# Retention and two routed expert layers on one core: output scaling and half of the masks move to ScalarE and GpSimd, logits are issued later, and SyncE's queue in the expert part is reordered

## The chip, the cores and the metric

The kernel runs on one core of one Trainium2 chip, as one program in one launch. The metric is device time in microseconds (us) of an execution; less is better. The engines of the core are TensorE (PE in the rows; PEld is its weight loads), VectorE (DVE), ScalarE (ACT), GpSimd (POOL) and SyncE (SP), which only issues DMAs. SBUF is the memory on the chip, PSUM the accumulators that matmuls write.

## The reference

Three layers follow each other: a retention without softmax, a layer of 8 experts, and a second layer of 8 experts. Each of the 4608 rows goes through one expert of each layer, chosen by the largest logit.

```python
# q, k, v: (B=8, H=8, S=576, 64) f32
scores = (1/8) * q @ k.T;  gamma_h = 1 - 2**(-5-h)
ret = scores * where(i >= j, gamma_h ** (i-j), 0)
x = (ret @ v), laid out as rows (B*S = 4608, D = 512)
# twice, with 8 experts, w1 (512, 1024), w2 (1024, 512):
logits = x @ w_gate          # the second layer adds modality_bias[modality_id]
e = argmax(logits);  p = softmax(logits)[e]
y = p * (relu(x @ w1[e]) @ w2[e])   # the first layer times sigmoid(x @ w_output_gate)[e] too
x = y
```

## The kernel before, in words

**Stage 1, attention and routing** (`attention_and_routing`). Retention is computed by chunks of 128 positions with a state per head. A batch element has four chunks and a half one; two elements share the half chunks as one joint tile, the tail. So there are 4 pairs x (4 + 4 + 1) = 36 chunks of 128 rows. For each chunk these steps run (names of `PLAN`, engine and line in brackets): the scaling of v (`vs`, GpSimd, L264); the scores of eight heads in two PSUM tiles `pa` of 128x512 (`S`, TensorE, L272); the product of q with the old state (`qS`, TensorE, L304); the new state's product (`kv`, TensorE, L279); the causal mask on each of the two score tiles (`am0`, `am1`, VectorE, L319); the state (`Sb`, VectorE, L288); the products of masked scores and v (`av0`, `av1`, TensorE, L304); the scaling of the output by a factor per row and head (`out`, VectorE, L326); the sum of squares of a row (`sq`, ScalarE, L330); a power of two from it as the row's scale (`rs1`, `rs2`, VectorE, L336 and L340); the row in float16 (`xh`, ScalarE, L345) and its rest in float16 (`xl`, VectorE, L348), which also issues a DMA transposition into `xT` on SyncE; and the router's logits from the transposed row (`lg`, TensorE, L357).

`PLAN` gives each step a time in chunks, counted from the chunk's own index; the program sorts all steps of all chunks by that time and emits them in this order, and each engine runs its own in order. Four to five chunks form a group of routing: when its last logits are due, `route` (VectorE mostly, with exponentials on ScalarE) steps forward every `STEP` of a chunk, and then GpSimd scatters the group's rows into the experts' buckets in DRAM (L170). Tiles of q, k, v are loaded by SyncE 4.5 chunks ahead, 256 KB each. `WEIGHTS` gives the times at which the 16 pieces (256 KB each, 128x512 float32) of the first expert's weights are converted, by ScalarE (L432) and VectorE (L433), into two float16 planes: the number and its rest. Their loads go through SyncE from chunk 30.3 on.

**Between the stages** the counts per expert go to registers (L405 to L415), a barrier waits for the scatters, and `experts` starts.

**Stage 2, the experts** (`experts`). Each engine has a program of its own, written out, with semaphores (`take` waits and counts down). The loop goes over 16 expert layers P, 8 of the first and 8 of the second layer. The rows of an expert come in slots: slot 0 and slot 1 are units of two blocks of 128 rows, then possibly more, then one odd block. For a unit SyncE transposes the rows into `xT` (L788), TensorE multiplies by the first weights (L947 to L949, three products of float16 planes), ScalarE and VectorE apply relu and split the result (L1046, L1155), TensorE multiplies by the second weights (L955 to L957), and ScalarE scales. In the first layer the rows of a finished block become rows `x2row`, SyncE transposes them to `x2T` (`turn`, L775), and in a later unit TensorE computes the second router's logits from them (L926), between the four quarters of the first product. The weights of the next expert come by SyncE (`load_w`, L760, four pieces of 1 MB into `stg`) and are converted by ScalarE (L1023) and VectorE (`stt`, shown with its helper's line L463) while this expert's products run. GpSimd scatters the rows of the second layer. At the start GpSimd clears the planes of `hT` (L1278).

SyncE's queue for an expert P is: slot 0's transposition, the `turn` of finished rows, slot 0's metadata; two pieces of the next expert's weights (`next_w(P+1, 1)`); then the same for slot 1, and so on; and at the end two pieces for the expert after (`next_w(P+2, 0)`).

## Time and profile before

| | |
|---|---|
| median of 3 runs | 1089.32 us (1088.02 to 1094.48) |
| the profiled execution | 1091.79 us, its span 1090.1 us |
| TensorE busy | 1003.2 us, 92% of the span |
| VectorE busy | 508.0 us, 47% |
| ScalarE busy | 329.5 us, 30% |
| GpSimd busy | 207.9 us, 19% |
| moved by DMA | 154.31 MB, 142 GB/s on average |
| mean granted TensorE clock | 0.964 |

All durations below are from the one profiled execution. A row of the timeline is one instruction, or a run of equal ones: start in us, duration in us, engine, line of the kernel, operation, output <- inputs, size, and how many (x16 are sixteen). What stands in brackets is how long the engine was idle before it, and what released it. The granted clock (PEclk) is a share of full speed: 1.00 is 2.4 GHz, 0.50 is 1.2 GHz. Stage 1 fills the first 247 us of the span, the first expert layer goes on to some 715 us, the second to the end.

### The profile page before, as it was taken

The page shows a single profiled execution, that of the slowest core. Times are in us where ns is not written, and L with a number is a line of the kernel's source. Part 1 is how long each engine was busy: PE and PEld are TensorE (multiplying, and loading weights), DVE is VectorE, ACT ScalarE, POOL GpSimd, SP SyncE. Part 2 cuts the span into 40 slices and gives each one's busy share as a digit, 9 for nine tenths or more (in the row PEclk, how much of TensorE's full clock was granted, in tenths as well). Part 3 has the DMA queues.
Part 4 walks back from the last instruction along what each step waited for, and adds up shares of the span by engine and source line. Part 5 has one row for each costly group of instructions (what it writes and reads, how often), then busy time and mean ns, then how long its engine had stood idle before and what let it go on. Part 6 is the DMA issues. An engine that isn't in the chain of part 4 may idle for free. (4 is left out here: it accounts for less than half of the span.)

```text
span 1090.1 us, 23903 instructions
## 1 busy us (share of the span) xinstructions
PE 1003.2 (92%) x8501; PEld 723.0 (66%) x8501; DVE 508.0 (47%) x1560; ACT 329.5 (30%) x637; POOL 207.9 (19%) x245
## 2 busy tenths in 40 slices
PE   7988988817999999999999899999999999999996
PEld 6977877705666767676666576766766766677664
DVE  5578798864555464646465646422311112111111
ACT  2222222332444443434344344313311121112111
POOL 4133333241111121212121213111001110110010
PEclk9799999957999999999999999999999999999998
DMA  9899999947765757574656584345122021311200
GB/s 292 233 251 269 257 273 281 278 128 228 197 152 144 156 134 167 133 157 125 162 136 153 135 167 134 80 135 134 49 59 58 29 61 40 63 55 39 58 29 32
DMA packets 218225, 154.31 MB, mean 142 GB/s; under 512 B 174665, under 2 KB 174829, under 8 KB 218096
## 3 DMA queue, kind: packets, MB, share of 16 engines
q1 hardware_dynamic: 209136, 124.09, 47.2%
q0 software_dynamic: 8960, 28.62, 7.5%
q8 instruction: 67, 1.10, 0.4%
q14 instruction: 62, 0.51, 0.2%
HBM read 80.21 MB, written 33.92 MB: 105 GB/s over the span
## 5 line engine op out<-in xcount | busy, mean ns | idle before, releaser
L947 PE MATMUL ph<-xT,wb 128*128 128x256 f16 (+2 forms) x1344 | 338.9, 263 | 19.7 <-PEq L451 19.7
L949 PE MATMUL ph<-xT,wb 128*128 128x256 f16 (+2 forms) x1344 | 339.0, 263 | 0.0
L948 PE MATMUL ph<-xT,wb 128*128 128x256 f16 (+2 forms) x1344 | 339.0, 263 | 0.0
L1155 DVE SCALAR_TENSOR_TENSOR hT<-ph,hT 128x512 f16<-128x512 f32 (+2 forms) x168 | 106.4, 637 | 333.7 <-DVEq L451 333.6
L955 PE MATMUL py<-wb,hT 128*128 128x512 f16 x608 | 230.6, 379 | 1.3 <-PEq L451 0.6
L956 PE MATMUL py<-wb,hT 128*128 128x512 f16 x608 | 230.5, 379 | 0.0
L957 PE MATMUL py<-wb,hT 128*128 128x512 f16 x608 | 230.4, 379 | 0.0
L1046 ACT ACTIVATE hT<-ph 128x512 f16<-128x512 f32 (+2 forms) x168 | 92.9, 553 | 224.2 <-ACTq L451 224.1
L947 PEld LDWEIGHTS ph<-xT,wb 128*128 128x128 f16 x1344 | 131.6, 98 | 37.6 <-issue 20.6
L948 PEld LDWEIGHTS ph<-xT,wb 128*128 128x128 f16 x1344 | 131.6, 98 | 17.0
L949 PEld LDWEIGHTS ph<-xT,wb 128*128 128x128 f16 x1344 | 131.7, 98 | 12.9
L957 PEld LDWEIGHTS py<-wb,hT 128*128 128x128 f16 x608 | 59.5, 98 | 72.0 <-issue 0.3
L955 PEld LDWEIGHTS py<-wb,hT 128*128 128x128 f16 x608 | 59.3, 98 | 66.9 <-issue 1.6
L956 PEld LDWEIGHTS py<-wb,hT 128*128 128x128 f16 x608 | 59.4, 98 | 64.9
L1273 POOL DMA_INDIRECT out_dram<-yo,idxo x37 | 36.0, 972 | 335.4 <-POOLq L451 322.3
L304 PE MATMUL po<-vs,a 128*128 128x64 f32 x576 | 80.5, 290 | 12.7 <-DVE a L319 12.4
L463 DVE SCALAR_TENSOR_TENSOR wb<-stg,wb 128x2048 f16<-128x2048 f32 x36 | 82.4, 2290 | 11.0 <-DVEq L451 11.0
L304 PEld LDWEIGHTS po<-vs,a 128*128 128x128 f32 x576 | 73.2, 202 | 15.8 <-DVE a L319 15.5
L1040 ACT ACTIVATE yo<-py,v_gcol 128x512 f32<-128x512 f32 x37 | 25.4, 687 | 168.3 <-ACTq L451 168.3
L1262 POOL TENSOR_SCALAR idx<-v_pos 128x1 int32<-128x1 f32 x39 | 10.5, 270 | 334.5 <-POOLq L451 334.5
L1023 ACT ACTIVATE wb<-stg 128x2048 f16<-128x2048 f32 x36 | 68.5, 1902 | 0.0
L319 DVE TENSOR_TENSOR a<-pa,mc 128x512 f32<-128x512 f32 x64 | 43.7, 685 | 42.1 <-PE pa L272 41.8
(154 smaller groups left out, 928.9 us busy)
## 6 DMA issues: line engine op xcount, KB each, us to landing
stg<-in_moe_w_dram SPq DMA_DIRECT2D x36, 1024.0 KB, 8.2
dkn<-in_dk_dram SPq DMA_DIRECT2D x36, 256.0 KB
qn<-in_q_dram SPq DMA_DIRECT2D x36, 256.0 KB
vn<-in_v_dram SPq DMA_DIRECT2D x36, 256.0 KB
kn<-in_k_dram SPq DMA_DIRECT2D x36, 256.0 KB
w0s<-in_moe_w_dram SPq DMA_DIRECT2D x16, 256.0 KB
xs<-zero SPq DMA_DIRECT2D x8, 262.0 KB, 2.2
xs<-zero SPq DMA_DIRECT2D x8, 258.0 KB, 2.8
```

Of the source, the lines that this page charges most:

```text
L304: nc.tensor.matmul(o, a, b_, start=m in fresh, stop=ends.get(m) == n)
L319: nc.vector.tensor_tensor(d4, s4, self.causal(), op=ALU.mult)
L463: r = fn(*a, **kw).then_inc(self.sem, 1)
L947: pe.matmul(o, w1(P_, 0)[:, c, fs], xT[s][:, c, cs], start=(c == 0), stop=False)
L948: pe.matmul(o, w1(P_, 0)[:, c, fs], xT[s][:, 4 + c, cs], start=False, stop=False)
L949: m = pe.matmul(o, w1(P_, 1)[:, c, fs], xT[s][:, c, cs], start=False, stop=(c == 3))
L955: pe.matmul(py[b], hT[:, 0, f, bs], w2(P_, 0)[:, f, :], start=(f == 0), stop=False)
L956: pe.matmul(py[b], hT[:, 0, f, bs], w2(P_, 1)[:, f, :], start=False, stop=False)
L957: m = pe.matmul(py[b], hT[:, 1, f, bs], w2(P_, 0)[:, f, :], start=False, stop=(f == 7))
L1023: ac.activation(wb[P_ % 2][:, 0, 2048 * c:2048 * c + 2048], stg[:, 2048 * c:2048 * c + 2048], AF.Copy, scale=WS).then_inc(T["cv_full"])
L1046: ac.activation(hT[:, 0, 2 * g:2 * g + 2, cs], ph[g][:, :, cs], AF.Relu).then_inc(T["hh_full"])
L1155: stt(hT[:, 1, 2 * g:2 * g + 2, cs], ph[g][:, :, cs], 0.0, hT[:, 0, 2 * g:2 * g + 2, cs], op0=ALU.max, op1=ALU.subtract).then_inc(T["h_full"])
```

## The change

It has four parts.

1. *Stage 1, engines.* `out` becomes eight ScalarE instructions, one per head, 128x64 each, that read the product in PSUM and scale by the head's column of factors. The mask of the second score tile (`am1`, not in tails) becomes a ScalarE copy out of PSUM and a GpSimd AFFINE_SELECT in place (`cut`), which fills zeros above the diagonal; tails and the first score tile keep the multiplication. The exponent `iv` is computed for a group in `route` instead of for each chunk.
2. *Stage 1, order.* `am1`, `out`, `sq`, `rs1` and `lg` have other times; `lg` moves from 3.6 to 4.1.
3. *Between the stages.* Only the first weights of expert 0 are loaded and converted in stage 1. The second weights follow in stage 2: SyncE loads them in two pieces of 1 MB behind the first unit's transposition, ScalarE and VectorE convert them in unit 0 after its first two quarters, and TensorE waits for each (`w0_full2`, `w0_full3`). SyncE issues the first transposition before it reads its other registers. TensorE runs 11 matmuls of constants (`READY`) ahead of the experts. The steps of the second router, which had nothing to do in the first unit, are left out there, with the clearing that they needed.
4. *Stage 2, SyncE's queue.* Slot 1's transpositions come ahead of `next_w(P+1, 1)`. For expert 0, two pieces of expert 1 go out ahead of slot 1 and two behind it, and the writes of padding come after slot 2. The counting of rows for the order of the second layer stands behind the second product instead of within it.

```diff
 PLAN = {
-    "vs": -1.3, "S": 0.0, ... "am0": 0.2, "am1": 0.35, "Sb": 0.5, "av0": 0.8, "av1": 0.85, "out": 1.25,
-    "sq": 1.3, "rs1": 1.65, "rs2": 1.75, "xh": 1.8, "xl": 2.25, "lg": 3.6,
+    "vs": -1.3, "S": 0.0, ... "am0": 0.2, "am1": 0.25, "cut": 0.4, "Sb": 0.5, "av0": 0.8, "av1": 0.85, "out": 1.35,
+    "sq": 1.4, "rs1": 1.7, "rs2": 1.75, "xh": 1.8, "xl": 2.25, "lg": 4.1,
 }
-WEIGHTS = 39.36, 39.38, 39.68, 39.83, 43.38, 44.04, 44.13, 45.14, 52.52, 59.82, 70.32, 70.53, 71.67, 73.74, 109.54, 132.91
+WEIGHTS = 39.36, 39.38, 39.68, 39.83, 43.38, 44.04, 44.13, 45.14
+READY = 11
...
 def route(gr):
...
+        v.tensor_scalar(iv[:, g].bitcast(I32), gr.eb[:, g], 8388608.0, 59.0 * 8388608.0, op0=ALU.mult, op1=ALU.add)
...
 def a_full(self, r):
...
-            nc.vector.tensor_tensor(d4, s4, self.causal(), op=ALU.mult)
+            if r == 0 or self.tail:
+                nc.vector.tensor_tensor(d4, s4, self.causal(), op=ALU.mult)
+            else:
+                nc.scalar.activation(self.aa[r], self.pa[r], AF.Copy)
+
+        def a_cut(self):
+
+            d4 = self.aa[1].rearrange("p (h i) -> p h i", h=4)
+            nc.gpsimd.affine_select(out=d4, in_=d4, pattern=[[0, 4], [1, C]], compare_op=ALU.is_ge, fill=0.0, base=0, channel_multiplier=-1)
...
         def out(self):
...
-            nc.vector.tensor_tensor(self.xg.rearrange("p (h d) -> p h d", h=H), self.po, col(f"gx{self.c}").unsqueeze(2).to_broadcast([P, 8, HD]), op=ALU.mult)
+            for h in range(H):
+                nc.scalar.activation(self.xg[:, h * HD:(h + 1) * HD], self.po[:, h, :], AF.Identity, scale=col(f"gx{self.c}")[:, h:h + 1])
...
         def row_scale2(self):
...
-            v.tensor_scalar(self.of("iv").bitcast(I32), self.of("eb"), 8388608.0, 59.0 * 8388608.0, op0=ALU.mult, op1=ALU.add)
...
     def registers(rs, eng, tag, names, full=None):
...
-        count1(eng, R_, 0)
+        if full:
+            eng.reg_load(R_["np"][0], reg1[0:1, 0:1])
+            with when(eng, R_["np"][0], "GT", 1):
+                full()
+            eng.reg_load(R_["od"][0], reg1[0:1, 8:9])
+        else:
+            count1(eng, R_, 0)
...
             # SyncE, at the start and for each expert
+                for c in (2, 3):
+                    load_w(0, c)
...
                         unit(P_, 0, lambda: row(0))
-                        next_w(P_ + 1, 1)
                         co.unlikely(pairs, "NE", 2, other, after)
                         unit(P_, 1, lambda: row(1))
+                        next_w(P_ + 1, 1)
...
                     if P_ == 0:
-                        for c in range(4):
+                        for c in range(2):
                             load_w(1, c)
...
                     if P_ == 0:
-                        pads(reg1, 16, xs1, "pad1", range(1, E))
+                        for c in (2, 3):
+                            take(sp, "stg_free")
+                            load_w(1, c)
...
             # TensorE
+                    if P_ == 0:
+                        pe.wait_ge(T["w0_full2"], 1)
                     second(0, range(4))
...
+                    if P_ == 0:
+                        pe.wait_ge(T["w0_full3"], 1)
                     second(0, (4, 5))
...
+                for n in range(READY):
+                    pe.matmul(py[1], K["ones"], K["ones"].unsqueeze(1).to_broadcast([P, 4, P]), start=True, stop=True)
...
             # ScalarE and VectorE, unit 0
+                        if P_ == 0 and slot == 0 and g < 2:
+                            conv(0, 2 + g)
```

The order of instructions shows what this does to the engines' queues. A row has the line, the operation, output <- inputs and the shape; the number in a name is its tile's.

ScalarE at two chunks in the middle of stage 1, before: `sq` and `xr` of one chunk stand behind each other.

```order
L330 ACTIVATE sq_0_1238,ss_127<-xg_0_1234 128x512
L345 ACTIVATE xr_131<-xg_0_1234,sc_129 128x512
L330 ACTIVATE sq_1_1311,ss_127<-xg_1_1309 128x512
L345 ACTIVATE xr_131<-xg_1_1309,sc_129 128x512
```

The same place now; `a_1_1` is the second score tile of the next chunk, `po` the product in PSUM, `xg` the scaled output.

```order
L324 ACTIVATE a_1_1_1316<-pa_1_1_1279 128x512
L337 ACTIVATE xg_0_1325<-po_0_1268,cst 128x64 x8
L341 ACTIVATE sq_0_1334,ss_127<-xg_0_1325 128x512
L222 ACTIVATE en_1321<-z_1320 128x5
L355 ACTIVATE xr_131<-xg_0_1325,sc_129 128x512
L324 ACTIVATE a_2_1_1405<-pa_2_1_1368 128x512
L337 ACTIVATE xg_1_1408<-po_1_1288,cst 128x64 x8
```

Per chunk, a copy of 512 columns and eight instructions of 64 have been put ahead of the squares, and the copy of the next chunk's scores stands ahead of this chunk's output.

GpSimd in the chunk loop, before: the scalings of v (L264) and between them the scatters of the rows of a group (L170).

```order
L264 TENSOR_TENSOR vs_1_1499<-vn_1_1249,cst 128x512
L264 TENSOR_TENSOR vs_2_1576<-vn_2_1324,cst 128x512
L170 DMA xs<-xr_126,pi_1508 40960x524
L264 TENSOR_TENSOR vs_3_1651<-vn_3_1410,cst 128x512
L170 DMA xs<-xr_126,pi_1508 40960x524 x3
L264 TENSOR_TENSOR vs_0_1727<-vn_0_1486,cst 128x512
```

The same group's scatters now, with `a_n_1` the tile that is masked in place.

```order
L266 TENSOR_TENSOR vs_2_1693<-vn_2_1427,cst 128x512
L329 AFFINE_SELECT a_1_1_1747<-a_1_1_1747 128x512
L266 TENSOR_TENSOR vs_3_1776<-vn_3_1520,cst 128x512
L171 DMA xs<-xr_126,pi_1664 40960x524 x2
L329 AFFINE_SELECT a_2_1_1828<-a_2_1_1828 128x512
L266 TENSOR_TENSOR vs_0_1856<-vn_0_1602,cst 128x512
L171 DMA xs<-xr_126,pi_1664 40960x524 x2
```

A mask of the loop now stands in GpSimd's queue behind scatters that wait for the positions of an earlier group.

TensorE at the logits of the fourth chunk, `pl`, before: they stand between `po <- Sb`, the product with the old state of a chunk three further on, and that chunk's products with masked scores, `po <- vs, a`.

```order
L304 MATMUL po_2_605<-Sb_103,qn_2_318 128x128 x4
L279 MATMUL pS_2_610<-vs_2_514,kn_2_322 64x64 x8
...
L357 MATMUL pl_442<-wg_94,xT_3_555 128x48
...
L304 MATMUL po_2_605<-vs_2_514,a_2_0_619 128x64 x4
L304 MATMUL po_2_605<-vs_2_514,a_2_1_628 128x64 x4
```

The same logits now.

```order
L306 MATMUL po_3_707<-Sb_104,qn_3_393 128x128 x4
...
L367 MATMUL pl_488<-wg_94,xT_3_584 128x48
...
L281 MATMUL pS_3_720<-vs_3_611,kn_3_397 64x64 x8
L306 MATMUL po_3_707<-vs_3_611,a_3_0_729 128x64 x4
L306 MATMUL po_3_707<-vs_3_611,a_3_1_734 128x64 x4
```

They have moved one chunk further: behind the products of the chunk above, and behind the next chunk's scores and `po <- Sb`; that chunk's state product now comes after them.

SyncE at an expert of the first layer, before: behind slot 0's transposition, turns and metadata come two pieces of weights, then slot 1's transposition and its turns (of the three alternative branches with 1, 2 and 2 turns one is taken).

```order
L792 DMA meta<-xs 128x2x12
L760 DMA stg<-in_moe_w_dram 128x4x512 x2
L572 COMPARE_AND_BRANCH
L788 DMA_TRANSPOSE xT<-xs 128x8x256
L551 COMPARE_AND_BRANCH x2
L611 UNCONDITIONAL_BRANCH
L775 DMA_TRANSPOSE x2T<-x2row 128x8x128
```

The same expert now.

```order
L816 DMA meta<-xs 128x2x12
L579 COMPARE_AND_BRANCH
L812 DMA_TRANSPOSE xT<-xs 128x8x256
L558 COMPARE_AND_BRANCH x2
L618 UNCONDITIONAL_BRANCH
L798 DMA_TRANSPOSE x2T<-x2row 128x8x128
...
L816 DMA meta<-xs 128x2x12
L783 DMA stg<-in_moe_w_dram 128x4x512 x2
L579 COMPARE_AND_BRANCH
L836 ISA
```

The two pieces of weights have gone behind slot 1's transposition, turns and metadata.

## Rows read from the trace of the kernel before

**Rows 1.** Windows: us, busy and (instructions) PE PEld DVE ACT POOL, PEclk, DMA share, GB/s
```profile
20.00:220.00 200.00, 174.11 (x2046) 157.81 (x2045) 153.30 (x435) 55.68 (x129) 62.06 (x59) 0.92 1.00 263
180.00:200.00 20.00, 17.54 (x229) 15.63 (x228) 17.51 (x49) 6.04 (x15) 3.95 (x4) 1.00 1.10 302
252.90:257.30 4.40, 4.34 (x21) 3.14 (x22) 0.00 (x0) 0.00 (x0) 0.00 (x0) 0.50 0.93 301
```

**Rows 2.** Timeline of TensorE: scores of four chunks, and one wait for logits
```profile
6.97 1.16 PE L272 MATMUL pa<-qn,dkn 64*128 64x128 f32 x16 [0.50 <-DMA qn<-in_q_dram]
...
27.63 0.37 PE L357 MATMUL pl<-wg,xT 128*128 128x48 bf16 x8 [3.92 <-DMA xT<-xr]
...
90.46 1.16 PE L272 MATMUL pa<-qn,dkn 64*128 64x128 f32 x16
...
95.43 1.16 PE L272 MATMUL pa<-qn,dkn 64*128 64x128 f32 x16
...
212.43 1.16 PE L272 MATMUL pa<-qn,dkn 64*128 64x128 f32 x16
```

**Rows 3.** Timeline of all engines from 97 us, and one row at 112.82
```profile
97.23 2.27 DVE L348 SCALAR_TENSOR_TENSOR xr<-xg,sc,xr 128x512 f16<-128x512 f32 x1
...
97.90 1.05 POOL L264 TENSOR_TENSOR vs<-vn,cst 128x512 f32<-128x512 f32 x1
...
99.43 0.68 DVE L326 TENSOR_TENSOR xg<-po,cst 128x512 f32<-128x512 f32 x1
...
100.76 1.10 PE L304 MATMUL po<-vs,a 128*128 128x64 f32 x8 [1.23 <-DVE a L319]
...
112.82 0.74 DVE L348 SCALAR_TENSOR_TENSOR xr<-xg,sc,xr 128x512 f16<-128x512 f32 x1
```

**Rows 4.** Waits, 40 to 205 us: engine line <- released by: us, times, longest
```profile
POOL xs L170 <- ACT xr L345: 49.7, 5, 10.8
...
PE po L304 <- DVE a L319: 11.6, 16, 1.2
```

**Rows 5.** Waits of the first expert layer, 255 to 720 us
```profile
PE pl L926 <- PEq L451: 10.5, 8, 2.1
```

**Rows 6.** Lines of ScalarE, 40 to 380: count | busy, mean ns | idle before, released by
```profile
L345 ACT ACTIVATE xr<-xg,sc 128x512 f16<-128x512 f32 x32 | 23.1, 722 | 25.2 <-DVE sc L340 22.2 <-issue 2.9
L330 ACT ACTIVATE sq<-xg 128x512 bf16<-128x512 f32 x32 | 20.2, 630 | 106.5 <-DVE xg L326 33.3 <-DVE pre L204 20.5 <-DVE se L219 19.1
```

**Rows 7.** Timeline of GpSimd at the making of the constants
```profile
1.62 0.28 POOL L96 TENSOR_SCALAR_AFFINE_SELECT mc<-ones 128x128 f16<-128x128 f16 x1
```

**Rows 8.** Timeline of ScalarE at the second router's exponential
```profile
371.89 0.30 ACT L1029 ACTIVATE w_ex<-w_l,v_nmx 128x8 f32<-128x8 f32 x1
372.10 0.18 ACT L1029 ACTIVATION_READ_ACCUMULATOR w_ex<-w_l,v_nmx 128x1 f32 x1
```

**Rows 9.** Timeline between the stages: last scatter, and TensorE's first expert matmul
```profile
241.43 0.98 POOL L170 DMA_INDIRECT xs<-xr,pi  x1 [0.30 <-issue]
...
252.96 0.37 PE L947 MATMUL ph<-xT,wb 128*128 128x256 f16 x1 [19.74 <-PEq L451]
```

**Rows 10.** Page, costliest groups, and DMA issues: KB each, us to landing
```profile
L463 DVE SCALAR_TENSOR_TENSOR wb<-stg,wb 128x2048 f16<-128x2048 f32 x36 | 82.4, 2290 | 11.0 <-DVEq L451 11.0
...
L1023 ACT ACTIVATE wb<-stg 128x2048 f16<-128x2048 f32 x36 | 68.5, 1902 | 0.0
...
stg<-in_moe_w_dram SPq DMA_DIRECT2D x36, 1024.0 KB, 8.2
```

**Rows 11.** Timeline of SyncE, VectorE and TensorE around a wait at L926
```profile
360.82 8.51 SPq L788 DMA_TRANSPOSE xT<-xs  x1
...
367.55 0.74 DVE L463 SCALAR_TENSOR_TENSOR x2row<-py,v_s,x2row 128x512 f16<-128x512 f32 x1
...
369.73 1.64 SPq L775 DMA_TRANSPOSE x2T<-x2row  x1
...
375.35 0.35 PE L926 MATMUL pl<-wg,x2T 128*128 128x24 bf16 x8 [2.08 <-PEq L451]
```

More of the change, by code (lines that the diff above doesn't have):

```diff
@@ L648, in without @@
                     none()
+                if first and P_ == 0:
+                    first()
+                for q in range(2 if conv and P_ == 0 else 0):
+                    conv(0, 2 + q)
                 if conv:
@@ L712, in routed, with behind @@
                         fn(1)
+    def behind(P_, slot):
+        return P_ < E and (P_, slot) != (0, 0)
     def note(eng, was, s, sure):
@@ L940, in unit @@
                     if routing is None:
-                        routing = P_ < E
+                        routing = behind(P_, slot)
                     def quarter(g):
@@ L1301, in _ @@
                     ahead(po, R_, P_)
-                    walk(co, R_, P_, unit)
+                    walk(co, R_, P_, unit, first=nothing)
                 co.end()
```

65 lines of the change are left out of this document (39 added, 26 removed).

## The prediction

> **What bounds the kernel now.** I read the windows first, then TensorE's timeline, the chunk loop and its waits, the change of stage and the experts. In the attention stage, 20 to 220 us [rows 1], TensorE is busy for 174 of 200 us at a granted clock of 0.92, VectorE for 153, and the DMA engines have a share of 1.00: three resources lie close together and none is full. TensorE's rows [rows 2] give the loop: the scores of the first chunk start at 6.97 us, those of the 36th at 212.43, so 205.5 us for 35 steps, 5.87 each. A step at full clock without a wait, from 90.46 to 95.43, takes 4.97, and 35 of those make 174. So 31.5 us lie above TensorE's own work: waits, such as the 3.92 at 27.63, and stretches at half clock (the mean of 0.92) that follow some of them.
>
> [rows 3] show how such a wait is made. While GpSimd scales v (97.90), `x_lo` on VectorE takes 2.27 us, where it takes 0.74 elsewhere (112.82). The output scaling (L326) and the second mask multiplication (L319) stand behind it in VectorE's queue, and TensorE has waited 1.23 us for that mask when it goes on at 100.76. Over 40 to 205 us this is TensorE's longest wait, 11.6 us in 16 times [rows 4].
>
> The experts are another regime, one matmul stream with few holes. The largest is 10.5 us in 8 times before the second router's matmuls, L926 [rows 5], for a transposed tile.
>
> **The change, part by part.**
>
> *The mask of the odd heads* leaves VectorE: ScalarE copies the scores, GpSimd masks them in place. For the copy I take the 0.63 us of `sq`, which has 128x512 too [rows 6]. An AFFINE_SELECT of 128 columns takes 0.28 us [rows 7]; for 512 that bounds the mask by 0.28 and 4 x 0.28 = 1.12, and I take the upper end, since it runs over all columns. From the start of a chunk's scores they end at 1.16 [rows 2], the copy near 1.8, the mask near 2.9; TensorE wants the odd product near 4.0 (4.97 less the last product's 1.0 [rows 3]). So 1.1 us are to spare where there was a wait.
>
> *The output scaling* becomes eight ScalarE instructions of 128x64 with a scale vector. `xr` has such a vector and takes 0.722 for 512 columns [rows 6], the exponential 0.30 for 8 [rows 8]: 0.84 ns a column, an estimated 0.35 for 64. The instruction behind the exponential starts 0.21 after it [rows 8], so eight take 8 x (0.35 - 0.09) = 2.1 us if they overlap like that, and 2.8 if they don't. On VectorE it was one of 0.68. ScalarE's step is then 0.63 (copy) + 2.1 + 0.63 (`sq`) + 0.7 of waiting for the row scale (22.2 us in 32 times) + 0.72 (`xr`) = 4.8 us, or 5.5 at the upper bound, against TensorE's 4.97. The Trainium skill, "ScalarE: Activation LUTs", What ACT_TABLE_LOAD costs, speaks against such a split: each ACTIVATE pays 186 ns, and 93 more for a pointer operand, before its columns, of which 93 overlap back to back. By it eight cost 8 x 0.24 = 1.9 us and the step 4.6; the rows show the same fixed part and carry the sum.
>
> *Logits later* (3.6 to 4.1). On TensorE they move from before a chunk's two products to behind the next chunk's scores and state product: 2 x 1.0 + 2 x 1.1 = 4.2 us. That covers the 3.92 at 27.63 and the half clock behind it. The exponent `iv`, once per group instead of per chunk, costs the last group's chain some 0.2.
>
> *Sum of the loop.* At most the 31.5 us could go. The DMA engines stop it earlier: at the share of the fullest window, 1.10 [rows 1], the 200 us become 182, and eight 256 KB weight loads less (2.1 MB at 302 GB/s) make it 175: -25. From below, the work put on ScalarE and GpSimd makes waits of its own: 0, or +5. Every engine's step fits, two of them barely, so I take the middle of -25 and 0: **-13**.
>
> *The change of stage.* The last scatter goes out at 241.43, a barrier waits until it has landed, the first expert matmul starts at 252.96 [rows 9], and TensorE runs at half clock for 4.4 us more [rows 1], worth 2.1. Now eleven filler matmuls run in the pause (-2.1), the first tile's transposition is issued before the register loads (an estimated -0.5), but the last output takes 2.1 on ScalarE instead of 0.68 (+1.4). Fewer conversions next to the scatters I take at nothing; two scatters' time (0.98 each) is the bound, -2. The second weights of expert 0 are now loaded after the barrier, issued some 2 us before TensorE's start, near 251: 8.2 us to landing, 1.9 and 2.29 of conversion [rows 10] make 263.4. TensorE, started at 252.5, wants them 10.5 later, at 263.0: +0.4. The second half lands some 3 us behind with its products 2.6 us behind: within the same. Sum **-1** (bounds -5 and +4, loads 3 us late).
>
> *The experts.* SyncE's queue now has the second slot's transpositions ahead of the next weights. In [rows 11] the router's tile was written by 368.29; its transposition went out at 369.73, since SyncE was held for 8.51 us by the one issued behind 2 MB of weights; TensorE waited 2.08 until 375.35. Issued at 368.3 it is 1.44 earlier. Six of the eight waits are of this kind, one per expert, 1.1 to 2.1 us each; cut by 1.44 at most they give 8.1, and all 10.5 if the tile, alone on the queues, also lands sooner. From below nothing, if issuing sooner doesn't land sooner. I take **-9.5**. The weights themselves go out some 10 us later, but their conversion comes 20 us after that.
>
> Total: -13 - 1 - 9.5 = -23.5. The profiled execution took 1091.8 us (span 1090.1), 2.5 above the median of 1089.3: 1068.3 on its scale, **1065.8** on the median's.
>
> **Rivals.**
> 1. *GpSimd becomes the loop's gate.* For: it sat idle at scatters for 49.7 us in 5 waits, up to 10.8, for positions that came late [rows 4], and masks now stand behind scatters; and a mask can hold `x_lo` as the scaling of v did, with the next state behind it. Against: it could wait so long only because it had run ahead; now the masks keep it in step, and to its 62 us in 200 [rows 1] some 35 come. Its price is the loop's 13: -10.5, 1079. The Trainium skill, "GPSIMD Engine Reference", Specifications, has the second half as a rule: its SBUF interfaces are shared with VectorE, in contention with VectorE's instructions of two SBUF inputs. By it `x_lo` waits behind each mask, and the 2.27 us agree.
> 2. *The experts' waits stay*, the landing rules: -14, 1075. Against it stand the 1.44 us that SyncE was late.
> 3. *Neither gains*: -1, 1088.
> 4. *Slower.* A scatter waits for positions longer than the masks' slack of 1.1 us, in each of 8 groups, and TensorE waits w and falls to half clock, worth about the 2.1 us of [rows 1]. At w = 3 that is 8 x 5.1 = 41; with no other gain in the loop, 41 - 10.5 = +30, 1120. It decides from w = 0.6 on (8 x 2.7 = 21.4, for +10.9).
>
> **How the numbers follow.** The forecast has 0.57, the rivals 0.20, 0.12, 0.06 and 0.05. The range goes from the bounds met together (-25 - 5 - 10.5 = -40.5, 1049, a little widened for the DMA cap) to short of the third rival: 1047 to 1084; beyond it lie the slower case, most of the third and a little of the first two. A measurement of this kernel can tell about 1%, 10.9 us, from no change. Faster by that: the forecast but for 0.01, half of the first rival, 0.11 of the second: 0.77. Slower 0.05, the fourth. Between: 0.18.
>
> **What would show it.** The 36th scores start near 199 us. ScalarE's output instructions follow each other by about 0.26. TensorE's waits for masked scores and for the loop's transposed rows are mostly gone, and with them the half clock between 28 and 43. The first expert matmul runs at full clock. L926's waits in the experts come to under 2.5 us. I am wrong if masks end later than 4 us after the scores' start, if GpSimd stands at a scatter with a mask behind it, or if the router's tile lands as late as before although it is issued earlier.

## The result and the profile after

The changed kernel takes 1054.91 us (median of 4 runs, 1051.01 to 1060.79), beside 1091.90 of the kernel before in the same series (4 runs, 1088.02 to 1099.96). The ratio is 0.9651, 95% interval 0.9609 to 0.9694: faster by 3.5%. Forecast were 1065.8 and a range of 1047 to 1084. The direction and all three places of the gain were right; the gain came out at 37 us (38.4 in the profiled executions) where 23.5 were forecast. Medians and ratios, here and below, are of executions in the faster of the two states that the times fall into; only run 5 had one in the slower, 1079.74 us, which its median leaves out.

Where it is, by the starts of TensorE's rows in the two profiled executions (us; the loop goes from the first scores to the scores of the 36th chunk):

| | first scores | loop | 36th scores to last product's end | to the first expert matmul | from there to the end | span |
|---|---|---|---|---|---|---|
| before | 6.97 | 205.46 | 6.28 | 34.25 | 837.09 | 1090.1 |
| after | 7.31 | 183.85 | 4.80 | 30.22 | 825.51 | 1051.7 |
| difference | +0.3 | -21.6 | -1.5 | -4.0 | -11.6 | -38.4 |
| forecast | | -13 | | -1, with the filler | -9.5 | -23.5 |

The windows of the changed kernel (columns as in [rows 1]): the steady part of the attention stage, and the first stretch of the experts.

```profile
20.00:190.00 170.00, 163.52 (x2032) 151.91 (x2031) 110.37 (x327) 125.17 (x420) 87.57 (x87) 0.95 1.08 290
226.20:230.00 3.80, 3.80 (x34) 3.33 (x33) 0.00 (x0) 0.65 (x2) 0.00 (x0) 0.93 1.04 400
```

The first ends at 190, since the last product is over at 195.96 now. TensorE is busy for 163.5 of its 170 us, the DMA engines have a share of 1.08 and move 290 GB/s; VectorE went down, ScalarE to more than twice what it had. The second answers to the last of [rows 1]: the experts start at a granted clock of 0.93 instead of 0.50.

One chunk in the timeline of the changed kernel, all engines, from its scores to the next chunk's; ahead of it a mask of the start of the program.

```profile
17.79 0.64 POOL L329 TENSOR_SCALAR_AFFINE_SELECT a<-a 128x512 f32<-128x512 f32 x1 [2.64 <-ACT a L324]
...
73.28 1.16 PE L274 MATMUL pa<-qn,dkn 64*128 64x128 f32 x16
...
74.58 0.60 ACT L324 ACTIVATE a<-pa 128x512 f32<-128x512 f32 x1
...
75.08 0.74 DVE L358 SCALAR_TENSOR_TENSOR xr<-xg,sc,xr 128x512 f16<-128x512 f32 x1
75.20 1.74 ACT L337 ACTIVATE xg<-po,cst 128x64 f32<-128x64 f32 x8
75.25 1.07 POOL L329 TENSOR_SCALAR_AFFINE_SELECT a<-a 128x512 f32<-128x512 f32 x1 [2.84 <-ACT a L324]
75.31 2.17 PE L306 MATMUL po<-vs,a 128*128 128x64 f32 x16
...
76.29 1.06 POOL L266 TENSOR_TENSOR vs<-vn,cst 128x512 f32<-128x512 f32 x1
...
77.41 1.16 PE L274 MATMUL pa<-qn,dkn 64*128 64x128 f32 x16
```

Read it as a relay. The copy starts 1.30 us after the scores' start, the mask follows it and ends at 76.32, 3.0 after the scores' start, and the sixteen products run through without a hole. The scaling of v comes right behind the mask, at 76.29, when the rest of x (75.08 to 75.82) is over.

The lines of the loop, 20 to 205 us, and the waits in it (columns as in [rows 6] and [rows 4]):

```profile
L324 ACT ACTIVATE a<-pa 128x512 f32<-128x512 f32 x30 | 17.9, 597 | 23.0 <-PE pa L274 22.7
L329 POOL TENSOR_SCALAR_AFFINE_SELECT a<-a 128x512 f32<-128x512 f32 x30 | 30.6, 1020 | 74.1 <-ACT a L324 73.7
L337 ACT ACTIVATE xg<-po,cst 128x64 f32<-128x64 f32 x280 | 60.8, 335 | 0.1
L358 DVE SCALAR_TENSOR_TENSOR xr<-xg,sc,xr 128x512 f16<-128x512 f32 x36 | 26.9, 746 | 1.0 <-ACT xr L355 1.0
```

```profile
PE pl L367 <- DMA xT<-xr: 13.0, 7, 3.2
...
POOL xs L171 <- DVE xr L236: 9.0, 3, 8.1
...
POOL xs L171 <- DVE sc L351: 1.6, 1, 1.6
```

TensorE waits for no mask any more (11.6 us in [rows 4]); all that is left are transposed rows, 13.0 us in 7: 6.5 us in four waits in the loop, and 6.5 in three behind the last product. GpSimd's 49.7 us at scatters are gone: the longest, 8.1, is the end of the stage.

The change of stage in the timeline (last scatter, first transposition, filler, first expert matmul) answers to [rows 9]:

```profile
215.37 0.98 POOL L171 DMA_INDIRECT xs<-xr,pi  x1 [0.30 <-issue]
221.12 1.92 SPq L760 DMA_TRANSPOSE xT<-xs  x1
...
221.54 4.85 PE L1030 MATMUL py<-ones 128*128 128x512 f16 x11 [12.11 <-issue]
...
226.18 0.42 PE L982 MATMUL ph<-xT,wb 128*128 128x256 f16 x1
```

From the last scatter to the first expert matmul it takes 10.81 us instead of 11.53, and the filler fills the last 4.85.

TensorE's waits in the first expert layer, 226 to 690 us, and one turn of the second router's tile (columns as in [rows 5] and [rows 11]):

```profile
PE pk L966 <- PEq L458: 7.0, 10, 1.9
...
PE pl L961 <- PEq L458: 1.7, 2, 1.4
```

```profile
338.63 0.74 DVE L470 SCALAR_TENSOR_TENSOR x2row<-py,v_s,x2row 128x512 f16<-128x512 f32 x1
...
339.55 1.23 SPq L798 DMA_TRANSPOSE x2T<-x2row  x1
...
343.98 0.35 PE L961 MATMUL pl<-wg,x2T 128*128 128x24 bf16 x8
```

The 10.5 us of [rows 5] have become 1.7. The tile is written by 339.37, its transposition goes out 0.18 later (1.44 in [rows 11]), and the logits run without a wait.

### The profile page after: what moved, and what is told of

Same layout as the page of the kernel before. It is cut to its first block, busy times and chain, and to the rows that moved or that the text cites. A ratio compares the mean times of both kernels' runs of the same rounds, so it can differ in the third digit from the quotient of the medians.

```text
span 1051.7 us, 24042 instructions
## 1 busy us (share of the span) xinstructions
PE 996.5 (95%) x8502; PEld 719.8 (68%) x8502; DVE 463.6 (44%) x1445; ACT 404.6 (38%) x948; POOL 232.8 (22%) x277
## 5 line engine op out<-in xcount | busy, mean ns | idle before, releaser
L470 DVE SCALAR_TENSOR_TENSOR wb<-stg,wb 128x2048 f16<-128x2048 f32 x38 | 87.0, 2290 | 11.7 <-DVEq L458 11.7
L1312 POOL TENSOR_SCALAR idx<-v_pos 128x1 int32<-128x1 f32 x39 | 16.1, 412 | 324.3 <-POOLq L458 324.3
L306 PE MATMUL po<-vs,a 128*128 128x64 f32 x576 | 76.1, 287 | 2.2 <-POOL a L329 2.2
L306 PEld LDWEIGHTS po<-vs,a 128*128 128x128 f32 x576 | 70.8, 199 | 4.6 <-POOL a L329 2.4
L1066 ACT ACTIVATE wb<-stg 128x2048 f16<-128x2048 f32 x38 | 72.3, 1902 | 0.0
L1077 ACT ACTIVATE sq<-py 128x512 bf16<-128x512 f32 x39 | 23.3, 597 | 111.7 <-ACTq L458 111.7
```

Of the source, the lines that this page charges most:

```text
L306: nc.tensor.matmul(o, a, b_, start=m in fresh, stop=ends.get(m) == n)
L470: r = fn(*a, **kw).then_inc(self.sem, 1)
L1066: ac.activation(wb[P_ % 2][:, 0, 2048 * c:2048 * c + 2048], stg[:, 2048 * c:2048 * c + 2048], AF.Copy, scale=WS).then_inc(T["cv_full"])
```

## The experiments

All start from the changed kernel. Each series of runs had its own runs of the kernel before, so ratios are compared, not times. "Loop" is that of the table above, from the profiled execution.

| kernel | median us | ratio to before, interval | loop | rest of x, mean |
|---|---|---|---|---|
| changed | 1054.91 | 0.9651, 0.9609 to 0.9694 | 183.9 | 0.75 |
| 1 logits early | 1065.60 | 0.9726, 0.9666 to 0.9787 | 197.7 | 0.78 |
| 2 mask on VectorE | 1058.41 | 0.9655, 0.9594 to 0.9716 | 191.3 | 1.07 |
| 3 output on VectorE | 1058.69 | 0.9665, 0.9605 to 0.9726 | 185.8 | 0.75 |
| 4 both on VectorE | 1071.17 | 0.9787, 0.9719 to 0.9856 | 200.3 | 0.90 |
| 5 SyncE's queue back | 1068.97 | 0.9730, 0.9663 to 0.9797 | 185.9 | 0.75 |
| 6 second weights in stage 1 | 1054.28 | 0.9634, 0.9590 to 0.9679 | 182.3 | 0.75 |
| 7 no filler | 1058.25 | 0.9664, 0.9619 to 0.9708 | 189.3 | 0.75 |
| 8 v scaled by ScalarE | 1060.22 | 0.9690, 0.9635 to 0.9746 | 189.5 | 0.74 |
| 9 logits later | 1052.99 | 0.9644, 0.9583 to 0.9705 | 185.5 | 0.89 |
| 10 and first mask | 1048.69 | 0.9604, 0.9542 to 0.9667 | 181.1 | 0.90 |
| 11 scatters packed | 1075.32 | 0.9862, 0.9798 to 0.9925 | 203.2 | 0.74 |

The loops of the changed kernel and of runs 5 and 7 are the same program: 183.9, 185.9 and 189.3. So a loop is known to some 5 us from one profile, and differences of that size are not read from it alone. Run 12 stands outside the table, since its rows go to other experts.

**1. The logits back to where they were.**

```diff
-    "sq": 1.4, "rs1": 1.7, "rs2": 1.75, "xh": 1.8, "xl": 2.25, "lg": 4.1,
+    "sq": 1.4, "rs1": 1.7, "rs2": 1.75, "xh": 1.8, "xl": 2.25, "lg": 3.6,
```

> The changed kernel with the logits back at 3.6, all else as changed. In the trace of the changed kernel the transposed rows land 0.5 to 7.3 us ahead of their logits, in 18 of 36 chunks by less than 3.7; at 3.6 the logits come about 4.2 us earlier on TensorE. Theory A (the later logits carry most of the loop's 21 us): waits for transposed rows of 1 to 3 us in most chunks, stretches at half clock behind them, the loop 12 to 20 us longer, 1067 to 1075 in all. Theory B (the relief of VectorE carries it): rows are ready earlier than before the change, so few waits, the loop 0 to 4 us longer, 1055 to 1059.

The loop is 13.8 us longer and TensorE waits for transposed rows (waits, 20 to 205 us):

```profile
PE pl L367 <- DMA xT<-xr: 13.8, 11, 2.9
```

This is theory A's forecast for the loop, from the slowest of the four executions; the total, 1065.60, lies between the two theories, and by the ratios (0.9726 and 0.9651) the early logits cost some 8 us. With them the engines still give 205.5 - 197.7 = 7.8 us of the loop, so theory B has a part too.

**2. The mask back on VectorE.**

```diff
-    ... "am1": 0.25, "cut": 0.4, ...
+    ... "am1": 0.35, ...
...
-            if r == 0 or self.tail:
-                nc.vector.tensor_tensor(d4, s4, self.causal(), op=ALU.mult)
-            else:
-                nc.scalar.activation(self.aa[r], self.pa[r], AF.Copy)
+            nc.vector.tensor_tensor(d4, s4, self.causal(), op=ALU.mult)
```

> The changed kernel with the mask of the second score tile back on VectorE at 0.35 (no ScalarE copy, no GpSimd select); output scaling stays on ScalarE. Theory A (the logits carry the gain): 0.69 us more per chunk on VectorE, which is idle for a third of the loop now; the mask ends at 1.16 + 0.69 + 0.69 = 2.5 us after the scores' start, earlier than the GpSimd mask's 3.0: the loop -2 to +2, 1053 to 1057. Theory B (VectorE's relief): the mask comes late behind the rest of x again as in the kernel before, 12 us of waits in the loop return in part, +5 to +12, 1060 to 1067.

The total, between the two theories' ranges, can't be told from the changed kernel's; the loop of the profile is 7.4 us longer than the changed kernel's, but only 2.0 longer than run 7's, which has the same stage 1. What returned is of theory B's kind (waits, and the line of the rest of x):

```profile
PE po L306 <- DVE a L321: 7.2, 7, 1.9
```

```profile
L355 DVE SCALAR_TENSOR_TENSOR xr<-xg,sc,xr 128x512 f16<-128x512 f32 x34 | 36.2, 1064 | 0.5 <-ACT xr L352 0.5
```

The rest of x takes 1.06 us again, although nothing about it was changed. In this kernel 12 of its 36 overlap a scaling of v on GpSimd and take 1.71 on average, up to 3.27; the other 24 take 0.74. In the kernel before they were 15 (1.58, up to 2.27) and 21 (0.74); in the changed one none overlaps. Without masks GpSimd is bound to nothing in the loop and its scaling falls on the rest of x by chance; with masks it runs right behind the mask, and the mask is bound to the scores. GpSimd's waits at scatters show the same: 47.8 us in 6, up to 10.8, without masks here, as in the kernel before.

**3. The output scaling back on VectorE.**

```diff
-    ... "out": 1.35,
-    "sq": 1.4, "rs1": 1.7, ...
+    ... "out": 1.25,
+    "sq": 1.3, "rs1": 1.65, ...
...
-            for h in range(H):
-                nc.scalar.activation(self.xg[:, h * HD:(h + 1) * HD], self.po[:, h, :], AF.Identity, scale=col(f"gx{self.c}")[:, h:h + 1])
+            nc.vector.tensor_tensor(self.xg.rearrange("p (h d) -> p h d", h=H), self.po, col(f"gx{self.c}").unsqueeze(2).to_broadcast([P, 8, HD]), op=ALU.mult)
```

> The changed kernel with the output scaling back on VectorE (one instruction of 0.68 us at 1.25, squares at 1.3, exponent at 1.65); the mask stays on ScalarE and GpSimd. Theory A: VectorE takes 0.68 more per chunk, ScalarE 1.74 less; x is ready about 1 us earlier, so transposed rows land earlier: the loop -4 to +1, 1051 to 1056. Theory B (VectorE's relief carries the gain): first masks (VectorE) queue behind the scaling, +4 to +12, 1059 to 1067.

No difference that can be told: the ratio is 0.9665, the loop 1.9 us longer, within its spread. By itself, on top of the other parts, this part of the change brings nothing that these runs can show.

**4. Both back on VectorE.** The diffs of 2 and 3 together.

> The changed kernel with both the mask and the output scaling back on VectorE: in stage 1 only the later logits and the per-group exponent are left of the change. Theory A: the loop stays within 5 us of the changed kernel's 183.9, 1055 to 1060. Theory B: the loop returns to 200 and more, 1070 to 1076; the rest of x on VectorE (0.75 us each in the changed kernel, 1.10 before) is stretched again by the scaling of v on GpSimd.

The loop is 200.3 and the waits for masks are back (20 to 205 us):

```profile
PE po L306 <- DVE a L321: 12.6, 10, 2.1
PE pl L363 <- DMA xT<-xr: 1.9, 1, 1.9
```

Theory B's number, then, where run 1 gave theory A's. Neither is right alone: two things make TensorE wait in a chunk, a late mask and late transposed rows, and each part of the change takes away one of them. In the kernel before both stand beside each other (waits, 20 to 218 us):

```profile
PE po L304 <- DVE a L319: 12.4, 17, 1.2
PE pl L357 <- DMA xT<-xr: 11.9, 11, 3.9
```

These are 24.3 us; run 4 has 14.5, run 1 has 13.8, and the changed kernel's loop 6.5: 9.8 less by later logits, 10.5 less by the engines, 17.8 less by both. So the waits fall by no more together than apart. The loops do: 205.5 - 200.3 = 5.2 us by later logits on the old engines, 7.8 by the engines with early logits, 21.6 by both. The difference lies in the time at half clock (the granted clock of the loop is 0.93 before, 0.90 and 0.91 in runs 4 and 1, 0.94 now) and in profiles of one execution each. The ratios of the totals do not bear it out: run 1 costs some 8 us by them and run 4 some 15, together about the 21.6. That the parts bring more together than apart is not shown.

**5. SyncE's queue of the experts as before.**

```diff
...
                         unit(P_, 0, lambda: row(0))
+                        next_w(P_ + 1, 1)
                         co.unlikely(pairs, "NE", 2, other, after)
                         unit(P_, 1, lambda: row(1))
-                        next_w(P_ + 1, 1)
```

> The changed kernel with SyncE's queue of experts 1 to 7 and of the second layer as before: two pieces of the next expert's weights ahead of slot 1's transposition and turns. Stage 1 and expert 0's own order stay as changed. Theory A (the router's tile waits in SyncE's queue, so issuing it sooner lands it sooner): the waits before the second router's matmuls, 1.7 us in 2 in the changed kernel, come back to some 9 us in 7, and the time from the first expert matmul to the end grows from 825.5 by 7 to 9, total 1062 to 1064. Rival (the counting moved behind the second product, or the time at half clock after the start, made the gain): the waits stay under 4 us and the stage within 2, 1055 to 1057.

The experts take 843.1 instead of 825.5 us, 17.5 more, in the slowest of the three executions that are compared (1061.53 to 1072.54); by the ratios (0.9730 and 0.9651) the old queue costs some 9 us, theory A's number. The waits, and one of them in the timeline:

```profile
PE pl L959 <- PEq L458: 17.2, 9, 2.9
```

```profile
285.50 0.74 DVE L470 SCALAR_TENSOR_TENSOR x2row<-py,v_s,x2row 128x512 f16<-128x512 f32 x1
...
287.23 2.88 SPq L798 DMA_TRANSPOSE x2T<-x2row  x1
...
294.03 0.37 PE L959 MATMUL pl<-wg,x2T 128*128 128x24 bf16 x8 [2.81 <-PEq L458]
```

The tile is written by 286.24 and issued 0.99 later; the logits start 6.8 us after the issue, where in the changed kernel 4.4 after it was in time. Being issued late is the smaller part: the tile also lands late. The six waits behind weights in the kernel before show the same. There the tile goes out 0.17 to 1.63 us after it is written, 0.8 on average, and the logits start 5.7 us after that; the same six tiles now go out after 0.17, and the logits start 4.7 after, without a wait. So some 0.7 us of each way comes from the issue, and at least 1.0 from the landing. Theory A holds in kind, more for the place in the queue than for the moment of issue. That the waits are longer than those of the kernel before (10.5) was not expected: the old order of experts 1 to 7 meets a changed order in expert 0 here, the six tiles go out 1.0 us after they are written and their logits start 6.3 after that, and why it is worse stays open.

**6. The second weights of expert 0 in stage 1 again.** The eight loads and conversions of the kernel before come back (`WEIGHTS` of 16 entries), the two 1 MB loads behind the barrier and TensorE's two waits go.

> The changed kernel with the second weights of expert 0 loaded (8 more pieces of 256 KB) and converted in stage 1 at the times of the kernel before, and no loads or conversions of them behind the barrier. Theory A (DMA caps the loop, as the prediction's bound of -25 had it): the eight loads cost up to 2.1 MB at 302 GB/s, 7 us of the loop, 1060 to 1062. Rival (they come after the loop's own loads, when the DMA queues have room, and only the conversions beside the last scatters count): the loop within 1.5 us, the time from the last product to the first expert matmul +1 to +2, 1055 to 1058.

The rival: the loop is 182.3, so the eight loads cost it nothing; they come behind its own loads. From the last product to the first expert matmul it takes 32.49 us instead of 30.22: three of the last scatters take 1.50 instead of 0.98 beside the conversions, and the last logits come 0.9 later behind the last product. The total can't be told from the changed kernel's.

**7. No filler matmuls.**

```diff
-READY = 11
+READY = 0
```

> The changed kernel without the 11 filler matmuls ahead of the experts. Theory A (they bring the clock up ahead of the first unit): the first expert matmul starts at about the same time, 30 us behind the last product, and TensorE runs at half clock for about 4.4 us more of the first unit, +2 us, 1057. Rival (the clock comes up anyway, or the start is set by the transposition alone): within 0.5 us.

The experts' first stretch is at half clock again (window; columns as in [rows 1]) and the time from the first expert matmul to the end is 826.98 instead of 825.51, +1.5:

```profile
230.80:234.80 4.00, 3.98 (x20) 2.79 (x21) 0.00 (x0) 0.00 (x0) 0.00 (x0) 0.51 0.98 362
```

In the runs with SyncE's queue as changed this time lies between 824.8 and 828.6, so it can't show 1.5 by itself. The rows can: the 21st matmul of the first unit starts 4.06 us after the first, where it was 2.45 with the filler, 1.6 sooner. So theory A holds, as read from the profile; the total (0.9664) can't show so little.

**8. v scaled by ScalarE, with mask and output on VectorE.**

```diff
-            nc.gpsimd.tensor_tensor(self.vs, self.heads("v"), col(f"gv{self.c}").unsqueeze(2).to_broadcast([P, 8, HD]), op=ALU.mult)
+            for h in range(H):
+                nc.scalar.activation(self.vs[:, h, :], self.heads("v")[:, h, :], AF.Identity, scale=col(f"gv{self.c}")[:, h:h + 1])
```

It is compared with run 4, from which it differs by this alone.

> Mask and output scaling back on VectorE as in the run before with both, later logits, and the scaling of v taken off GpSimd: eight ScalarE instructions with the head's factor, some 1.8 us a chunk on an engine that is busy for under a third of the loop there. GpSimd has only scatters and constants left in stage 1. Theory C (the masks on VectorE come late because GpSimd's scaling of v stretches the rest of x to 1.5 us on average and up to 2.8 where they overlap, 0.75 where not): the rest of x takes 0.75 throughout, the waits for masks fall from 12.6 us to under 4, and the loop from 200.3 to 186 to 191, total 1056 to 1062. Rival (VectorE's queue is too long in itself, with mask, scaling, x and routing in one line): the waits stay over 8 us, the loop at 196 or more, 1066 to 1072.

```profile
PE po L307 <- DVE a L322: 6.6, 10, 0.8
PE pl L364 <- DMA xT<-xr: 4.1, 2, 3.7
```

```profile
L355 DVE SCALAR_TENSOR_TENSOR xr<-xg,sc,xr 128x512 f16<-128x512 f32 x35 | 26.0, 744 | 3.4 <-ACT xr L352 3.3
```

The rest of x takes 0.744 throughout, the waits for masks fall from 12.6 us (longest 2.1) to 6.6 (longest 0.8), and the loop from 200.3 to 189.5. So VectorE keeps its whole load here, and most of what the masks' and outputs' move brought is reached by taking GpSimd's scaling out of its way: 10.8 us of the 16.4 between run 4 and the changed kernel. The waits fall only by half, where theory C had them under 4; the 6.6 that remain, ten of up to 0.8, are the part of the queue itself: theory C for the larger part of the loop, the rival for the rest.

**9 and 10. Logits later still, and the first mask on VectorE.**

```diff
 # run 9
-    ... "lg": 4.1,
+    ... "lg": 4.9,
 # run 10 as well
-            if r == 0 or self.tail:
+            if r == 0 or self.tail or self is order[0]:
...
         def a_cut(self):
 
+            if self is order[0]:
+                return
```

> The changed kernel with the logits at 4.9 instead of 4.1: on TensorE behind the two products of the chunk four further on, another 3 to 4 us later. Theory A (what is left of waits in the loop are transposed rows that land late, 5.7 to 9.9 us in 2 to 5 waits per execution so far, with half clock behind them): these waits go, the loop falls from 182 to 189 to 174 to 178, total 1045 to 1051. Rival (the DMA queues are full, so the wait only moves to the loads of q and k or to a free buffer for the transposition): the loop stays at 182 to 189, 1053 to 1057.

> As the run before, and the second mask of the very first chunk is put on VectorE. In the changed kernel GpSimd's first mask stands behind the scaling of the second chunk's v, which waits for its load; TensorE waits 2.25 us at 13.07 and then runs at half clock for 3.4 to 6.8 us. Theory A: the scores of the second chunk start 3 to 5 us earlier (14.97 in the changed kernel, 11.29 before), total 3 to 5 below the run before. Rival (the second chunk's loads set its start): 0 to 1.

Run 9 (waits, 20 to 205 us) shows the rival: as many transposed rows are late as before, the loop is 185.5, and the total the same. The five that are late in the loop go out 1.1 to 4.8 us after they are written, where it was at most 0.1 for the four in the changed kernel; SyncE's waits for earlier logits, which free a buffer, grow from 0.8 us in 2 to 9.2 in 5 (20 to 190 us).

```profile
PE pl L367 <- DMA xT<-xr: 10.8, 6, 2.7
```

Its rest of x takes 0.89 in the mean. In six chunks the order of two starts has turned round: the mask (or the scaling) comes first, and the rest of x stays until GpSimd's two are done, as in these rows of its timeline. The mask is all but over when the rest of x starts; it is the scaling right behind it that holds it, up to 0.55 us before the end of the rest of x.

```profile
98.86 0.64 POOL L329 TENSOR_SCALAR_AFFINE_SELECT a<-a 128x512 f32<-128x512 f32 x1
...
99.43 1.62 DVE L358 SCALAR_TENSOR_TENSOR xr<-xg,sc,xr 128x512 f16<-128x512 f32 x1
99.46 1.04 POOL L266 TENSOR_TENSOR vs<-vn,cst 128x512 f32<-128x512 f32 x1
```

Run 10 takes the wait away that the change had made at the start of the program (row of the changed kernel, then the second chunk's scores in run 10):

```profile
13.07 1.97 PE L306 MATMUL po<-vs,a 128*128 128x64 f32 x8 [2.25 <-POOL a L329]
14.97 2.08 PE L274 MATMUL pa<-qn,dkn 64*128 64x128 f32 x16
```

```profile
11.24 0.94 PE L274 MATMUL pa<-qn,dkn 64*128 64x128 f32 x12
```

The second scores start at 11.24 instead of 13.53 in run 9, the third at 16.31 instead of 19.84, and the total is 4.3 below run 9's, as forecast. At 1048.69 us, a ratio of 0.9604, it is the fastest of these kernels; against the changed kernel its interval (0.9542 to 0.9667) still overlaps.

**11. Scatters packed ahead of masks.**

```diff
-SCATTER = 0.225, 0.428
+SCATTER = 0.0, 0.01
```

> The changed kernel with all scatters of a group issued right behind its positions (0.0 and 0.01 in place of 0.225 and 0.428 of a chunk apart), so that four or five scatters of some 1.28 us, 5 to 6 us, and whatever they wait for positions stand ahead of one mask in each of 8 groups. In the changed kernel the mask ends 3.0 us after the scores' start and TensorE wants it near 4. Theory (rival 4 of the prediction, masks behind scatters hold TensorE): waits of 3 to 5 us for masked scores in 7 groups, each with half clock worth 2 or more, +30 to +45, 1085 to 1100. Rival (GpSimd has run ahead far enough that the mask is late by under 1 us): within 3 us, 1053 to 1058.

TensorE's waits, 20 to 212 us, and one of them on GpSimd and TensorE:

```profile
PE po L306 <- POOL a L329: 17.6, 6, 3.6
```

```profile
61.74 1.15 POOL L171 DMA_INDIRECT xs<-xr,pi  x1 [1.49 <-DVE xr L236]
...
65.84 0.98 POOL L171 DMA_INDIRECT xs<-xr,pi  x1 [0.30 <-issue]
66.83 1.06 POOL L266 TENSOR_TENSOR vs<-vn,cst 128x512 f32<-128x512 f32 x1
67.82 0.65 POOL L329 TENSOR_SCALAR_AFFINE_SELECT a<-a 128x512 f32<-128x512 f32 x1
```

```profile
68.53 1.97 PE L306 MATMUL po<-vs,a 128*128 128x64 f32 x8 [2.30 <-POOL a L329]
70.43 2.08 PE L274 MATMUL pa<-qn,dkn 64*128 64x128 f32 x16
```

The mechanism of the slower rival is there: six waits of 2.9 us on average and half clock behind each. The loop grows by 19.3 us and the total by some 23 by the ratio, not by 30 to 45. The waits for transposed rows go in exchange: none is left in the loop. That TensorE, held by masks, leaves the DMA queues more time is the likely reason (a share of 1.02 in this loop, 1.07 in the changed kernel's), but not shown apart. With the changed kernel's spacing of the scatters nothing of all this is seen.

**12. Without the loads of k.**

```diff
         def load(self, L):
+            if L == "k":
+                self.src[L] = self.src["q"]
+                return
```

> The changed kernel without the loads of k: the state's product takes q in its place, so that one of four loads per chunk (256 KB each, 9.4 MB in all) is left out and the output is another one; the instructions of all engines, the logits at 4.1 and the rest are as changed. The rows go to other experts, so only stage 1 is compared, not the total. Theory A (full DMA queues make the transposed rows late, and that is all that TensorE waits for in the loop): no waits for transposed rows over 1 us and no half clock between 25 and 190 us, the loop 174 to 178. Rival (the rows are late for the transposition's own time, or their place behind loads in SyncE's queue): waits of 5 us and more stay, the loop 181 to 189.

The window (columns as in [rows 1]) and the waits, 20 to 190 us:

```profile
20.00:190.00 170.00, 163.04 (x2106) 150.59 (x2105) 115.83 (x350) 132.09 (x444) 86.07 (x89) 1.00 0.99 245
```

```profile
PE po L309 <- DVE a L325: 3.1, 7, 1.1
PE pl L370 <- DMA xT<-xr: 1.2, 1, 1.2
```

In this one execution the loop takes 173.3 us, the granted clock stays at 1.00 from 20 to 190 us, and of the waits for transposed rows one of 1.2 is left. So full DMA queues are what the loop of the changed kernel still waits for, some 10 us. Fewer loads also leave SyncE more room, which this run by itself does not part from the DMA queues; the changed kernel's rows do. The four transpositions that TensorE waits for in its loop go out within 0.1 us of being written, and the logits start 8.6 to 11.2 us after the issue; of the last two, with the DMA engines at a share of 0.44 (196 to 204 us), 3.1 to 3.2. The 173.3 are also what 35 times the undisturbed step of [rows 2] gives, 174.

## Why the prediction was right, and where its sizes were off

**The loop: the mechanism was right, the term was sized -13 and measured -21.6.** Two sentences of the sum failed, in opposite directions.

The first is the choice of "the middle of -25 and 0", for waits that the new work on ScalarE and GpSimd would make. There are none between 20 and 205 us. The steps it rested on were nearly right: the mask ends 3.0 us after the scores' start (2.9 forecast), its length is 1.02 (1.12), ScalarE's eight instructions take 1.74 (2.1) and its chunk 3.9 of work and some 0.7 of waiting (4.1 and 0.7). The mask's length was met by luck: alone it takes 0.64, far below the 1.12 taken, and it comes to 1.02 for a reason that the text did not have, the rest of x. By these steps every engine had room within 4.97, as the text itself said; taking half of the gain off for it was caution without a row behind it. The one wait of the kind that does exist, 2.25 us in the first chunk, stood in no step.

The second is the DMA cap. The eight loads that were taken out of stage 1 were given 7 us of it; run 6 puts them back and the loop stays. But the cap is real: run 12 takes a quarter of the loads away and the loop falls by another 10.6. The share of 1.10 of the fullest window [rows 1] was a fair bound for the average (1.08 over 170 us now), and 182 the better cap: 183.9 was measured. That is in part luck, since the share by itself is no gauge of full queues: it was 1.00 in the kernel before [rows 1], with a longer loop, and is 0.99 in run 12, with a shorter one. So -25 was too far for the wrong reason and the middle too near.

Both kinds of wait that the text named, late masks and late rows, went with the part that was made for them (runs 1 and 4). The sum had no term for either part, so it can't be said which one it had too small.

**How the wait of [rows 3] was removed** was told in part wrongly. The prediction had VectorE's queue relieved of two instructions. Run 8 shows that the larger part, 10.8 of 16.4 us, was the overlap with GpSimd's scaling of v, which the text had read in [rows 3], and that the change removed it in a way the text did not see: by giving GpSimd a mask, which ties its scaling to a place where the rest of x is over.

**Rival 1**, GpSimd as the gate, is wrong in both halves. It waits at no scatter for more than 1.6 us in the loop (up to 10.8 before), because the masks keep it in step, as the "against" had it: without them it waits again, 47.8 us in run 2 and 62.1 in run 4. And the masks do not hold the rest of x: 30 of them overlap one, the rest of x takes 0.75 in the mean, and it is the mask that gets longer, 1.02 on average, 0.64 in the two at the start that stand alone. In all 30 the rest of x starts first, by 0.1 to 0.6 us: it waits for `xr` on ScalarE, the mask for the copy right behind `xr` in ScalarE's queue. Where a mask starts first, it holds it: in run 10 one mask starts at 121.80, 0.07 us ahead of the rest of x, which then takes 1.13; with the scaling right behind, 1.62 (run 9). So the rival's mechanism exists, and ScalarE's order keeps it away. The Trainium skill, "SBUF — State Buffer", SBUF: two separate sides, has it as a rule: whichever of the two starts first keeps the shared ports for its whole instruction. All 30 masks agree: each ends 0.49 us after the rest of x that it started behind. Of the seven scalings in the kernel before whose row starts while a rest of x runs only one does; in the other six, that of [rows 3] among them, the rest of x is slowed although its row starts first, and ends 0.56 after the scaling.

**Rival 4**, masks behind scatters, has the right mechanism (run 11) and does not happen at the change's spacing. Its price of 41 was too high, since it left out that the waits for transposed rows go in exchange. (Its 8 x 2.7 is 21.6, not 21.4; the 0.6 stays.)

**The change of stage: forecast -1, measured -5.5 and some 1.6 more in the first unit.** The filler's -2.1 and the second weights' +0.4 fall behind the first expert matmul, so for the stretch that measured -5.5 the text had some +1. The 5.5 are 1.5 from the 36th scores to the last product, 1.3 from there to the last logits, 2.0 on to the last scatter and 0.7 on to the first expert matmul. The step that failed is "fewer conversions next to the scatters I take at nothing". Run 6 gives 2.3 us for that and the loads with it, about what the text had as its bound, 2, though only half of it lies beside the scatters. The second is +1.4 for the outputs on ScalarE, which is not to be seen: the last logits come 7.9 us behind the last product instead of 9.2. The third is +0.4 for second weights that come late: TensorE does not wait for them at all. The filler brought some 1.6 (run 7) of the 2.1 forecast, and the transposition 0.7 (11.53 to 10.81) of 0.5.

**The experts: forecast -9.5, measured -11.6, of which the filler is some 1.6.** This step was right in place and size: the waits at the second router fall by 8.8 us, and run 5 brings them back with SyncE's order alone. Its way there was right in part. The 1.44 us by which SyncE was late in [rows 11] were taken for all six waits, but in three of them it was late by less than 0.5 (run 5 has the six); the larger part is the landing, which the text had only in its upper bound ("alone on the queues, also lands sooner"). So rival 2, that the landing rules, is right on what rules and wrong on the waits: issued sooner, the tile also goes ahead of 2 MB of weights, and lands sooner. The weights' later issue costs nothing that is seen; waits at the next matmul, the ranks (L931 before, L966 now), grow from 5.2 to 7.0 us.

**The sum.** -21.3 for the loop with its start, -5.5 and -11.6 give the 38.4 of the profiled executions. Had the loop been taken at the cap of 182 without the caution, -18, and the scatters at their bound, the sum would have been -30.5.

## What to carry to other kernels

Where one engine waits now for one and now for another thing in each turn of a loop, count each kind of wait by itself, give each a part of the change, and set the turn without any wait against the next limit, here the DMA queues. An engine that runs free beside a loop can hit its neighbours at a bad moment; giving it an instruction that depends on the loop's main engine ties its other work to a place, as long as the order of the starts there stays what it was (run 9). Transpositions whose result is wanted soon belong ahead of large loads in a queue, for the place on the DMA queues more than for the moment of issue.

## What the runs showed of the hardware

- A VectorE instruction with two SBUF inputs (the rest of x, 128x512) takes 0.74 us alone, 1.58 to 1.71 on average and up to 3.27 where GpSimd's multiplication of two SBUF inputs overlaps it. The two do not share, one waits for the other: in the kernel before 14 of 15 such instructions end 0.55 to 0.56 us after GpSimd's. An AFFINE_SELECT of the same size that starts after it leaves it alone, goes from 0.64 to 1.02 on average itself and ends 0.49 after it, 30 times of 30; one that starts 0.07 ahead of it makes it take 1.13 (run 10).
- Eight ScalarE instructions of 128x64 with a scale vector, back to back, take 1.74 us: 0.335 each, of which some 0.13 overlap the next, so that they start 0.20 apart (0.26 forecast).
- With the same instructions, the attention loop took 183.9, 185.9 and 189.3 us in three executions. The waits in it are for transposed rows on full DMA queues: logits that wait start 8.6 to 11.2 us after the issue, 3.1 to 3.2 behind the last product, with the DMA engines at a share of 0.44; without a quarter of the loads it took 173.3 at a clock of 1.00.
